# Attention then feed-forward on one core: weight loads spread behind normalizations, early v loads on another queue, and longer planned DMA times

## The chip, the cores and the metric

The kernel runs on one core of one Trainium2 chip. The metric is the device time of one execution in microseconds (us); the smaller the better. The engines are named as in the profile: PE is TensorE's matrix unit (PEld its weight loads), DVE is VectorE, ACT is ScalarE, POOL is GpSimd, SP is SyncE, which here only issues DMAs. ACTq, POOLq and SPq are their instruction queues. PSUM is the memory that matmuls write.

## What is computed

Attention with normalized q and k over 8 batches, 12 heads, 448 rows and 64 columns per head, and then a feed-forward layer with a gate over the 8 x 448 = 3584 rows of 768.

```
q, k, v: (8, 12, 448, 64)   w_in: (768, 2048)   w_out: (2048, 768)
q_n = q / sqrt(mean(q*q) + 1e-6) * g_q ;  k_n likewise with g_k
attn = softmax(q_n @ k_n.T / 8) @ v          # per batch and head
x = attn, heads side by side                 # (3584, 768)
h = x @ w_in
out = (h * clip(h + 3, 0, 6) / 6) @ w_out    # (3584, 768)
```

## The kernel before

**Tiling.** Two heads make a pair (index p, 48 in all; six pairs, HP, make one batch of x). Two pairs make a group (GP = 2), which is the unit of loading: `load_k` (L287), `load_q` (L278) and `load_v` (L294) bring one group's k, q or v, each as one large and one or two small DMAs, into one of NS staging buffers `kq_in` and `v_st`. The pairs of group 0 have k and q loaded one by one. The 448 rows of a head lie as three full tiles of 128 rows and a rest of 64; the rests of both heads share a tile.

**One pair's way.** `square` (L329) and `stats_sum` (L336) give the sums of squares, `stats_rstd` (L343) the factors, and `normalize` (L352) writes the scaled q and k as bf16 into `qk` (three tiles, NQ). Then q and k are transposed: for pairs below TD = 14 by PE into the PSUM tile `t_ps` (`transposes`, L364; k in its first half, q in the second), from which `put_k` and `put_q` (L381 to L388) copy them into `kq`; for later pairs by a transposing DMA on SP (`transposes_dma`, L376), after which ACT scales q (`scale_q`, L372). `burst` and `rests` (L390 to L405) make the scores, `expo2` (L407) their exponentials on ACT, `weigh` (L420) multiplies with v (cast to bf16 by `cast_v`, L359), and `divide` (L441) ends the softmax. The result is transposed into `xT`: below XD = 12 by PE (`x_out`, L462, into the PSUM tile `m` for the first batch) and `put_x` (L473), later by a transposing DMA (`x_out_dma`, L466).

**Feed-forward.** When the six pairs of a batch are in `xT`, the items `h` (`h_mm`, L478; six matmuls each, then `relu` on ACT and `gate` on DVE) and `y` (`y_mm`, L495; 16 matmuls each, a copy and a store) of that batch can run. One part of the first h item (`h_early`, L588) is spread over the pairs of the first batch.

**What sets the order.** A planner (`Plan`, L64) writes the whole order at build time. Each operation has a key (lower first), one or more engines with a planned duration, and dependencies. `run` (L140) steps through planned time; whenever an engine is free it gives it the ready operation with the lowest key. PE's matmuls of the feed-forward fill in between by `share` and `credit`. The engines and queues then execute exactly this order; on the chip an instruction waits for what it needs, and all behind it on its engine waits too. Planned times of DMAs are made of ISSUE (0.6 us on SP and ACT, 0.9 on POOL, per DMA), the bytes at RATE in one common pipe, and LAND until the data can be used. A transposing DMA is planned with 1.27 us of issue and a fixed time behind it (L95).

```
    def dma_transpose(self, key, size, fn, deps):
        return self.add(key, [("SP", 1270, fn)], deps, 2100, 1.4 * size)
```

**Loads.** k, q and v go through SP's queue (group 0's q through ACT's) in the order of their keys. A group's k and q wait, in the plan and on the chip, until the group NS before has been normalized, and its v until that one's v has been cast. The weights are nine DMAs on POOL's queue with a cast on the way: `load_w_in` (L312) for five ranges of columns, `load_w_out` (L316) for four. W_IN and W_OUT (L644) give for each the group whose v load it is planned behind: w_in 2, 2, 2, 3, 3 and w_out 5, 5, 6, 7. POOL also makes most normalizations (for all pairs but the first), most squares from pair 4 on and most casts of v.

Of the kernel before, what the change touches and what calls it, by code (L numbers as in the profile page):

```python
# [63 lines left out]
class Plan:  # L64
# [6 lines left out]
    ISSUE, LAND, RATE = {"SP": 600, "ACT": 600, "POOL": 900}, 1700, 270.0  # L71

    STEADY, SLACK, EARLY = 110e3, 500, 3000

    def __init__(self, share):
        self.free = {e: 0.0 for e in ("PE", "ACT", "DVE", "POOL", "SP", "pipe")}
        self.known, self.todo = [], 0
        self.lanes, self.row, self.banks = {"h": [], "y": []}, [], []
        self.share, self.credit = share, 0.0
# [15 lines left out]
    def dma_transpose(self, key, size, fn, deps):  # L95
        return self.add(key, [("SP", 1270, fn)], deps, 2100, 1.4 * size)
# [43 lines left out]
    def run(self):  # L140
        now = 0.0
        while self.todo or self.row or any(self.lanes.values()):
            soon = [t for t in self.free.values() if t > now]
            best = {}
            for op in self.known:
                t = op.time
                if op.bank is not None:
                    free = After(op.bank).end
                    if free is None:
                        continue  # L150
                    t = max(t, free + self.HOP)
                if t > now:
                    soon.append(t)
                    continue
                engine, ns, fn = min(op.ways, key=lambda w: max(self.free[w[0]], now) + w[1] * (
                    self.PRICE.get(w[0], 1.0) if op.key[0] >= self.FAIR else 1.0))
                if self.free[engine] <= now and (engine not in best or op.key < best[engine][0].key):
                    best[engine] = (op, ns, fn)
            if self.free["PE"] <= now and ("PE" not in best or self.credit < 0):
                if not self.row:  # L160
                    pick = self.next_item(now, soon)
                    if pick:
                        it, bank = pick
                        for lane in self.lanes.values():
                            if lane and lane[0] is it:
                                lane.pop(0)
                        it.bank, bank[1] = bank, it.out
                        self.row = list(it.ops)
                if self.row:
                    best["PE"] = (self.row[0], *self.row[0].ways[0][1:])  # L170
            if not best:
                now = min(soon)
            for engine, (op, ns, fn) in best.items():
                if op.key is None:
                    self.row.pop(0)
                    share = next((self.share[i] for i in range(0, len(self.share) - 1, 2)
                                  if it.place < self.share[i + 1]), self.share[-1])
                    self.credit = min(self.credit + ns * share, 2000.0)
                else:
                    self.known.remove(op)  # L180
                    self.todo -= 1
                    if engine == "PE":
                        self.credit = max(self.credit - ns, -2000.0)
                self.begin(op, engine, ns, fn, now)
        return now
# [3 lines left out]
def kernel(  # L189
# [11 lines left out]
    nc = tc.nc  # L201
# [13 lines left out]
    NS = 3  # L215
# [3 lines left out]
    TD = 14  # L219
    XD = 12  # L220
# [131 lines left out]
    def normalize(eng, p):  # L352
        eng.tensor_tensor(  # L353
            out=qk_r[p % NQ][:].rearrange("p a t h d -> p h (a t) d"), in0=raw(p, 2),
            in1=rstd_r[(p // GP) % 2][:, p % GP].rearrange("p h a t -> p h (a t)")
            .unsqueeze(3).to_broadcast([P, 2, 8, D]), op=A_MULT,
        )
# [6 lines left out]
    def transposes(p):  # L364
        for a in range(2):
            for t in range(4):
                nc.tensor.transpose(
                    t_ps[:, a, t * P:(t + 1) * P],
                    qk_r[p % NQ][:, a, t].rearrange("p h d -> p (h d)"), identity[:],
                )  # L370
# [10 lines left out]
    def put_q(eng, p):  # L381
        if eng is nc.scalar:
            eng.activation(out=qT_r[p % NK], in_=t_ps[:, 1, 0:S], func=COPY, scale=gprime[:])
        else:
            eng.tensor_scalar_mul(qT_r[p % NK], t_ps[:, 1, 0:S], gprime[:])

    def put_k(eng, p):
        copy(eng, out=kT_r[p % NK], in_=t_ps[:, 0, :])  # L388
# [67 lines left out]

    x_own = m_r[1][:].bitcast(BF16)
# [89 lines left out]
    V, G, A_ = nc.vector, nc.gpsimd, nc.scalar  # L547
    SINGLE = 4
# [6 lines left out]
    t_bank = []  # L555
    sc_last, ex_of, d_ops = {}, {}, []

    def x_stage(p):
# [10 lines left out]
        if p >= HP:  # L569
            xo[p].bank, xo[p].readers = t_bank, [px[p]]  # L570
# [69 lines left out]
    QA, VL, WK = 1, 1.5, 0  # L640
# [3 lines left out]
    W_IN = ((2, 0, 256), (2, 256, 256), (2, 512, 512), (3, 1024, 512), (3, 1536, 512))  # L644
    W_OUT = ((5, 0, 0, 8), (5, 0, 8, 8), (6, 1, 0, 8), (7, 1, 8, 8))
    w_loads, w_in_ops, w_out_ops = [], [], ([], [])
    for i, (after, *cols) in enumerate(W_IN):
        op = plan.dma((GP * after - WK, 3 + i), 1, NKT * P * cols[1] * 4, lambda cols=cols: load_w_in(*cols),
# [3 lines left out]
    for i, (after, *rows) in enumerate(W_OUT):  # L652
        op = plan.dma((GP * after - WK, 8 + i), 1, rows[2] * P * YC * 4, lambda rows=rows: load_w_out(*rows),
# [22 lines left out]
    for p in range(NPAIR):  # L676
        g = p // GP
        if p % GP == 0:
# [15 lines left out]
            lv_g[p] = plan.dma((p if g else VL, 2), 3, GP * kb, lambda p=p: load_v(nc.sync, p, GP), oldv)  # L694
            for i in range(1, GP):
                lv_g[p + i] = lv_g[p]
            for after, op in w_loads:
                if after == g:
                    lv_g[p].next.append(op)
            for i in range(GP):  # L700
                j, p0 = min(i, len(todo) - 1), p + i
                parts = []
                for part in ((0, 1) if p0 == 0 else (2,)):
# [10 lines left out]
                if g < SINGLE:  # L714
                    rstd_op[p0] = add((p0 - 2, 0), [("ACT", 430, lambda p0=p0: stats_rstd(
                        p0, (slice(None), p0 % GP)))], parts)
                else:
                    sums += parts
            if g >= SINGLE:
                rs = add((p - 2, 0), [("ACT", 450, lambda p=p: stats_rstd(p, (slice(None),)))],  # L720
                         sums[-GP:] + (norm_g[g - 2] if g >= 2 else []))
                for i in range(GP):
                    rstd_op[p + i] = rs
        ways = [("POOL", 1910, lambda p=p: normalize(G, p))]
        if p < 1:
            ways = [("DVE", 1240, lambda p=p: normalize(V, p))]
        nrm.append(add((p - 2, 4), ways, [rstd_op[p], at(tr, p - NQ)]))
        norm_g.setdefault(g, []).append(nrm[p])
        lv = lv_g
# [10 lines left out]
        else:  # L740
            free = sc_last.get(p - NK, [])
            tr.append(add((p - 1, 3), [("PE", 440, lambda p=p: transposes(p))],
                          [nrm[p], *free], 165))
            pq.append(add((p - 1, 3 if p == 0 else 0), [("DVE", 450, lambda p=p: put_q(V, p)), ("ACT", 640, lambda p=p: put_q(A_, p))],
                          [tr[p], mg]))
            pk.append(add((p - 1, 1), [("DVE", 420, lambda p=p: put_k(V, p)), ("ACT", 600, lambda p=p: put_k(A_, p))],
                          [tr[p]]))
            tr[p].bank, tr[p].readers = t_bank, [pq[p], pk[p]]
# [89 lines left out]
```

## Time and profile before

| | us |
|---|---|
| runs | 438.52, 441.98, 443.76 (median 441.98) |
| profiled execution | 439.38 |
| its span, first to last instruction | 437.6 |
| PE busy | 409.8 |
| ACT busy | 254.3 |
| DVE busy | 234.7 |
| POOL busy | 195.2 |
| bytes moved by DMA | 64.55 MB |

Busy time is what an engine's own instructions took; issuing a DMA, waiting and branching are not counted on SP's and ACT's queues. In a line of the timeline, the brackets give the engine's idle time before the instruction and what ended it. In the view by stretch, each engine has its busy time and, in parentheses, its number of instructions; then come the TensorE clock that was granted (1.00 is full speed), the mean busy share of the 16 DMA engines (some overlap makes it exceed 1), and GB/s. In the view of waits: who waited, for whom, us in total, times, longest us.

### The profile page before, as it was taken

What the parts mean: (1) busy time and instruction counts of PE and PEld (TensorE: products, weight loads), DVE (VectorE), ACT (ScalarE), POOL (GpSimd) and SP (SyncE); (2) the same over time, 40 slices, a digit from 0 to 9 for tenths busy, and PEclk for the clock granted to TensorE, in tenths of its full rate; (3) what the DMA queues carried; (4) which work ended last, traced back from release to release, by engine and by line L of the source; (5) the groups of instructions that cost most, each with busy time, mean ns of one, the idle gap of its engine ahead of it and who ended that gap; (6) DMA issues with size and microseconds to landing.
All of it is one profiled execution on the core that took longest, in us unless ns stands there. A gap on an engine that the chain in (4) does not pass through costs nothing.

```text
span 437.6 us, 8944 instructions
## 1 busy us (share of the span) xinstructions
PE 409.8 (94%) x3520; PEld 236.5 (54%) x3520; DVE 234.7 (54%) x492; ACT 254.3 (58%) x414; POOL 195.2 (45%) x146
## 2 busy tenths in 40 slices
PE   0677899999999998999999999999999999999997
PEld 0355565555566554555555555555565555555565
DVE  6486777766455557556466366344444253343322
ACT  3886887734877885968778587666643032132100
POOL 3697785596377776859676556311000000000000
PEclk9998999999999999999999999999999999999999
DMA  6999999995978898999999994333211201100022
GB/s 170 267 228 216 221 222 239 250 190 131 237 161 190 204 217 189 201 219 194 227 212 167 191 213 121 73 88 91 61 24 49 72 1 51 59 36 37 25 85 73
DMA packets 126506, 64.55 MB, mean 148 GB/s; under 512 B 77824, under 2 KB 123008, under 8 KB 126464
## 3 DMA queue, kind: packets, MB, share of 16 engines
q1 hardware_dynamic: 117488, 57.24, 57.5%
q0 software_dynamic: 8144, 6.29, 9.2%
q8 instruction: 27, 0.44, 0.4%
q10 hardware_dynamic: 832, 0.46, 0.4%
q14 instruction: 15, 0.12, 0.1%
HBM read 45.61 MB, written 11.01 MB: 129 GB/s over the span
## 4 chain that ended last, share of the span: by engine, by line
PE 82%; DMA 7%; ACT 3%; DVE 3%; SPq 2%; POOL 2%; issue 1%; ACTq 0%; POOLq 0%
PE m L479 18%; PE m L498 17%; PE t_ps L498 9%; PE t_ps L479 8%; PE av L435 7%; PE sc L395 6%; PE sc L498 6%; PE sc L479 4%; DMA kq_in<-in_k_dram 3%; DMA kq<-qk 3%; PE av L429 2%; DMA kq_in<-in_q_dram 2%; PE sc L402 2%; ACT eT L408 2%; DVE ssq L337 1%
## 5 line engine op out<-in xcount | busy, mean ns | idle before, releaser
L408 ACT ACTIVATE eT<-sc 128x896 bf16<-128x896 f32 x168 | 147.2, 915 | 42.2 <-PE sc L395 38.5
L498 PEld LDWEIGHTS <-gT 128*128 128x128 bf16 x912 | 85.5, 98 | 61.7 <-issue 8.9
L479 PE MATMUL m<-xT,w_in_sb 128*128 128x448 bf16 x486 | 109.9, 353 | 1.7 <-DVE xT L475 0.6
L479 PEld LDWEIGHTS <-w_in_sb 128*128 128x128 bf16 x768 | 70.7, 98 | 68.8 <-issue 12.0
L353 POOL TENSOR_TENSOR qk<-kq_in,rstd 128x1024 bf16<-128x1024 f32 x47 | 89.0, 1903 | 41.6 <-DMA kq<-qk 20.8
L498 PE MATMUL m<-w_out_sb,gT 128*128 128x384 bf16 (+1 forms) x480 | 87.3, 324 | 0.0
L334 POOL TENSOR_TENSOR sq<-kq_in 128x1024 f32<-128x1024 f32 x41 | 77.2, 1894 | 13.0 <-DMA kq_in<-in_q_dram 3.6
L490 DVE SCALAR_TENSOR_TENSOR gT<-t_sb,m 128x448 bf16<-128x448 f32 x81 | 49.9, 618 | 41.8 <-ACT t_sb L485 41.4
L485 ACT ACTIVATE t_sb<-m 128x448 f32<-128x448 f32 x81 | 44.1, 546 | 47.9 <-PE m L479 47.2
L337 DVE TENSOR_REDUCE ssq<-sq 128x16 f32<-128x1024 f32 (+1 forms) x49 | 58.1, 1190 | 9.5 <-POOL sq L334 7.5
L435 PE MATMUL av<-vaug,eT 128*128 128x65 bf16 x1152 | 59.6, 196 | 0.0
L435 PEld LDWEIGHTS <-eT 128*128 128x128 bf16 x1152 | 52.8, 100 | 7.2 <-issue 1.6
L498 PE MATMUL t_ps<-w_out_sb,gT 128*128 128x384 bf16 x256 | 46.9, 326 | 0.0
L395 PE MATMUL sc<-kq 64*128 64x448 bf16 x288 | 41.6, 363 | 4.0 <-ACT eT L408 2.5
L429 PE MATMUL av<-vaug,eT 128*128 128x130 bf16 x192 | 43.0, 224 | 2.4 <-ACT eT L408 1.2
L479 PE MATMUL t_ps<-xT,w_in_sb 128*128 128x448 bf16 x192 | 44.5, 352 | 0.7 <-DVE gT L490 0.7
L303 POOL CAST vaug<-v_st 128x512 bf16<-128x512 f32 x33 | 20.3, 620 | 55.0 <-PE av L435 46.6
L445 DVE RECIPROCAL rden<-av 128x4 f32<-128x4 f32 x96 | 17.3, 180 | 48.8 <-PE av L435 47.1
L446 DVE TENSOR_TENSOR xn<-av,rden 128x256 bf16<-128x256 f32 x96 | 40.7, 424 | 3.3
L374 ACT ACTIVATE kq<-kq,gprime 128x448 bf16<-128x448 bf16 x34 | 22.8, 670 | 14.2 <-DMA kq<-qk 14.2
L498 PE MATMUL sc<-w_out_sb,gT 128*128 128x384 bf16 (+1 forms) x176 | 29.1, 319 | 0.0
L485 ACT ACTIVATE t_sb<-t_ps 128x448 f32<-128x448 f32 x32 | 17.5, 547 | 19.7 <-PE t_ps L479 18.5
(50 smaller groups left out, 225.0 us busy)
## 6 DMA issues: line engine op xcount, KB each, us to landing
v_st<-in_v_dram SPq DMA_DIRECT2D x24, 384.0 KB, 4.7
kq_in<-in_k_dram SPq DMA_DIRECT2D x23, 384.0 KB, 4.5
kq_in<-in_q_dram SPq DMA_DIRECT2D x23, 384.0 KB, 4.8
out_dram<-y_sb SPq DMA_DIRECT2D x23, 384.0 KB, 2.6
w_out_sb<-in_moe_w_out_dram POOLq DMA_DIRECT2D x4, 768.0 KB, 19.1
w_in_sb<-in_moe_w_in_dram POOLq DMA_DIRECT2D x3, 768.0 KB, 16.2
out_dram<-y_sb SPq DMA_DIRECT2D x9, 192.0 KB, 2.7
v_st<-in_v_dram SPq DMA_DIRECT2D x48, 32.0 KB, 4.3
```

Source lines behind the costliest of these rows:

```text
L334: eng.tensor_tensor(out=sq, in0=x, in1=x, op=A_MULT)
L337: nc.vector.tensor_reduce(out=ssq_r[(p // GP) % 2][:, p % GP, :, which(part)].rearrange("p h a t -> p h (a t)"), in_=sq_r[m][:, :, which(p ...
L353: eng.tensor_tensor(out=qk_r[p % NQ][:].rearrange("p a t h d -> p h (a t) d"), in0=raw(p, 2), in1=rstd_r[(p // GP) % 2][:, p % GP].rearran ...
L395: nc.tensor.matmul(out=sc[:, h, 0:S], lhsT=kT_r[p % NK][rows, t * P:(t + 1) * P], rhs=qT_r[p % NK][rows], start=True, stop=True,)
L408: nc.scalar.activation(out=e2_r[d % NE][:, :, 0:S], in_=sc_r[i][:, :, 0:S], func=EXP, bias=0.0, scale=1.0,)
L429: nc.tensor.matmul(out=av, lhsT=rest[:, cols], rhs=va[:, 3].rearrange("p h d -> p (h d)"), start=True, stop=False, skip_group_check=True,)
L435: nc.tensor.matmul(out=av[:, h * W:(h + 1) * W], lhsT=e[t][h][:, cols], rhs=va[:, t, h], start=False, stop=(t == NT - 1 and h == 1), skip_ ...
L446: nc.vector.tensor_tensor(out=xn_r[p % NQ][:, t].rearrange("p n (h d) -> p n h d", h=2), in0=av4[:, :, :, 0:D], in1=rden.unsqueeze(3).to_b ...
L479: nc.tensor.matmul(out=m[:, 0:S], lhsT=w_in_sb[:, kt, f * P:(f + 1) * P], rhs=xT[:, kt, b % NX, x_slot(b)], start=(kt == 0), stop=(kt == N ...
L485: nc.scalar.activation(out=t[:], in_=m[:, 0:S], func=RELU, bias=0.5, scale=1.0 / 6.0,)
L490: nc.vector.scalar_tensor_tensor(out=gT[:, f, (b % 2) * S:(b % 2 + 1) * S], in0=t[:], scalar=1.0, in1=m[:, 0:S], op0=A_MIN, op1=A_MULT,)
L498: nc.tensor.matmul(out=m[:, 0:n], lhsT=gT[:, f, c0:c0 + P], rhs=w_out_sb[:, f, c:c + n], start=(f == 0), stop=(f == NFT - 1),)
```

## The change

- Each of the nine weight loads is planned and issued behind one pair's normalization: w_in behind pairs 3, 4, 5, 6 and 7, w_out behind pairs 7, 8, 9 and 10.
- v of groups 0 and 1 is issued by POOL rather than SP.
- Pair 0's normalization and factors are made for k and for q apart (SPLIT). For pairs 0 and 1 the transposes are two operations, and those of q go to the PSUM tile `m` that also takes the first batch's `x_out` (QB). Pair 0's k is copied by ACT and its q by DVE.
- There are four staging buffers rather than three.
- Planned times: a transposing DMA takes 3.5 us behind its issue rather than 2.1, a load lands 2.6 us behind the pipe rather than 1.7, the pipe has 300 bytes per ns rather than 270, and all engines start at 0.7 us.
- A new rule in `run`: an engine other than PE and SP is left idle when an operation whose key is lower by one or more becomes ready within half of the duration of the one that it would start. The choice between engines now also looks at when the operation becomes ready.

```diff
-    ISSUE, LAND, RATE = {"SP": 600, "ACT": 600, "POOL": 900}, 1700, 270.0
+    ISSUE, LAND, RATE = {"SP": 600, "ACT": 600, "POOL": 900}, 2600, 300.0
+    TURN = 3500
...
+    AHEAD, LOOK = 1, 0.5
...
-        self.free = {e: 0.0 for e in ("PE", "ACT", "DVE", "POOL", "SP", "pipe")}
+        self.free = {e: 700.0 for e in ("PE", "ACT", "DVE", "POOL", "SP", "pipe")}
...
-        return self.add(key, [("SP", 1270, fn)], deps, 2100, 1.4 * size)
+        return self.add(key, [("SP", 1270, fn)], deps, self.TURN, 1.4 * size)
...
+                engine, ns, fn = min(op.ways, key=lambda w: max(self.free[w[0]], now, t) + w[1] * (
+                    self.PRICE.get(w[0], 1.0) if op.key[0] >= self.FAIR else 1.0))
                 if t > now:
                     soon.append(t)
+                    ahead.append((engine, t, op.key))
                     continue
...
+            for engine, t, key in ahead:
+                if engine in best and engine != "PE" and engine != "SP":
+                    op, ns, _ = best[engine]
+                    if key[0] + self.AHEAD <= op.key[0] and t - now < self.LOOK * ns:
+                        del best[engine]
...
-    NS = 3
+    NS = 4
...
+    x_own = m_r[1][:].bitcast(BF16)
+    def t_place(p, a):
+        return x_own[:, 0:W4] if a and p < QB else t_ps[:, a, :]
...
-    W_IN = ((2, 0, 256), (2, 256, 256), (2, 512, 512), (3, 1024, 512), (3, 1536, 512))
-    W_OUT = ((5, 0, 0, 8), (5, 0, 8, 8), (6, 1, 0, 8), (7, 1, 8, 8))
+    W_IN = ((3, 0, 256), (4, 256, 256), (5, 512, 512), (6, 1024, 512), (7, 1536, 512))
+    W_OUT = ((7, 0, 0, 8), (8, 0, 8, 8), (9, 1, 0, 8), (10, 1, 8, 8))
...
-            lv_g[p] = plan.dma((p if g else VL, 2), 3, GP * kb, lambda p=p: load_v(nc.sync, p, GP), oldv)
+            veng, queue = (nc.gpsimd, "POOL") if g < VP else (nc.sync, "SP")
+            lv_g[p] = plan.dma((VK[g] if g < VP else p, 2), 3, GP * kb, lambda p=p, veng=veng: load_v(veng, p, GP), oldv,
+                               queue=queue)
...
-            for after, op in w_loads:
-                if after == g:
-                    lv_g[p].next.append(op)
...
-        nrm.append(add((p - 2, 4), ways, [rstd_op[p], at(tr, p - NQ)]))
+        ns = [normal(p, part, x) for part, x in zip((0, 1) if p < SPLIT else (2,), rstd_op[p])]
+        nrm.append(ns[-1])
         norm_g.setdefault(g, []).append(nrm[p])
+        for after, op in w_loads:
+            if after == p:
+                nrm[p].next.append(op)
+                op.deps[id(nrm[p])] = nrm[p]
...
+            ts = [add((p - 1, 3), [("PE", 440 if part == 2 else 220, lambda p=p, part=part: transposes(p, part))],
+                      [n, *free], 165) for part, n in ((0, ns[0]), (1, ns[-1]))[:2 if p < QB else 0] or ((2, nrm[p]),)]
+            tr.append(ts[-1])
...
+            ts[0].bank, ts[0].readers = t_bank, [pk[p]] + [pq[p]] * (p >= QB)
+            if p < QB:
+                ts[1].bank, ts[1].readers = x_own_bank, [pq[p]]
```

## Prediction

> **What bounds the kernel now.** The first view is the page: TensorE (PE) is busy for 409.8 of 437.6 us and the chain that ended last is 82% PE. No other engine passes 58%. PE's work does not change in this edit, so the time can only move by PE's idle time, 27.8 us, and the question is where that lies.
>
> ```profile
> span 437.6 us, 8944 instructions
> ...
> PE 409.8 (94%) x3520; PEld 236.5 (54%) x3520; DVE 234.7 (54%) x492; ACT 254.3 (58%) x414; POOL 195.2 (45%) x146
> ...
> PE   0677899999999998999999999999999999999997
> ...
> PE 82%; DMA 7%; ACT 3%; DVE 3%; SPq 2%; POOL 2%; issue 1%; ACTq 0%; POOLq 0%
> ```
>
> The second view, busy time by stretch, answers it. First column: length; second: PE busy; the last two: DMA share and GB/s.
>
> ```profile
> 0.00:9.38 9.38, 0.00 (x0) 0.00 (x1) 6.13 (x33) 3.87 (x6) 3.14 (x16) 1.00 0.59 161
> 9.38:52.41 43.03, 31.95 (x354) 20.20 (x355) 28.64 (x62) 33.20 (x54) 35.62 (x27) 0.96 1.08 233
> 52.41:150.00 97.59, 97.53 (x903) 56.62 (x903) 62.66 (x128) 67.47 (x111) 66.42 (x45) 1.00 0.97 203
> 150.00:232.00 82.00, 77.91 (x726) 43.90 (x724) 51.55 (x101) 62.33 (x105) 59.46 (x38) 1.00 0.99 210
> 232.00:435.00 203.00, 202.46 (x1541) 115.84 (x1538) 85.74 (x172) 87.42 (x140) 30.58 (x23) 1.00 0.33 79
> 435.00:437.60 2.60, 0.00 (x0) 0.00 (x0) 0.00 (x0) 0.00 (x0) 0.00 (x0) 1.00 0.13 41
> ```
>
> PE's idle time is 9.38 + 11.08 + 0.06 + 4.09 + 0.54 + 2.60 us. So there are two places where this edit can gain: the head, until the first batch's x is whole and feed-forward matmuls fill every gap (20.5 us), and the stretch 150 to 232 us (4.1 us). The rest is the last store.
>
> The third view is the chain of waits in order of time, for the head (start, length, what).
>
> ```profile
> 1.27 3.69 DMA kq_in<-in_q_dram
> 4.96 0.02 issue
> 4.98 0.59 SPq L298
> ...
> 9.52 4.37 DMA kq_in<-in_q_dram
> 13.89 0.33 issue
> 14.22 2.00 ACT sq L332 x2
> ```
>
> SP issues the first v loads (L298, L300) from 4.98 to 6.95, and only then k and q of the second group, whose squares start as q lands at 13.9. The timeline shows pair 0's two evacuations in turn, and the weights' loads in a row on POOL with what they do to SP's queue:
>
> ```profile
> 10.45 0.59 ACT L303 COPY kq<-t_ps 128x512 bf16<-128x512 bf16 x1 [1.38 <-PE t_ps L367]
> ...
> 11.07 0.45 DVE L385 TENSOR_SCALAR kq<-t_ps,gprime 128x448 bf16<-128x448 bf16 x1 [0.62 <-ACT kq L303]
> ...
> 28.72 2.54 POOL L313 DMA_DIRECT2D w_in_sb<-in_moe_w_in_dram  x3
> ...
> 36.97 4.77 SPq L292 DMA_DIRECT2D kq_in<-in_k_dram  x2
> ```
>
> For 150 to 232 us, the view of waits and that of the transposing DMA's line:
>
> ```profile
> ACT kq L374 <- DMA kq<-qk: 10.9, 8, 2.8
> ...
> POOL qk L353 <- DMA kq<-qk: 4.9, 4, 2.2
> ...
> DMA to landing us min/median/max: 3.1/3.6/6.0
> ```
>
> ACT and POOL work in a fixed order, and both stand for this DMA; behind ACT's 2.8 us (before 170.2) come the exponentials for which PE then waits.
>
> **The change, part by part.**
>
> *Pair 0 in two halves.* Today: sums 6.29 to 7.57 (two of 0.64), rstd to 8.06, one normalization of 1.23 to 9.33, eight transposes 9.38 to 10.41, k's copy (0.59), then q's (0.45), scores at 11.57. After: k's sum ends at 6.93 and its rstd (0.45) at 7.4; q's sum holds DVE until 7.57; half normalizations (0.62 each) end at 8.2 and 8.85; four transposes of k end at 8.75 and of q at 9.4; k's copy is hidden behind q's, which now lies in another PSUM bank, and q's ends at 9.9. Scores at 9.95: 1.6 us earlier. Added: two ACT instructions of 0.21, inside ACT's idle time.
>
> *v of groups 0 and 1 by POOL.* Six issues leave SP: 1.97 us (4.98 to 6.95) ahead of group 1's k and q, and 1.94 (10.17 to 12.11) ahead of group 2's. On POOL I price them by its nearest rows, 0.55 (gk_t) to 0.93 (w_out_sb): 3.3 to 5.6 us, hidden in the 8.4 us that POOL waited for v before its casts at 9.92 and 16.02; without that cover it would be late for pair 1's normalization by what exceeds it. But the bytes share the DMA engines. Between 0 and 5 us the share is 0.47 at 125 GB/s, between 5 and 10 0.76 at 217, afterwards 0.94 and up, to 267 GB/s. So 0.96 MB of room lies before 10 us, 3.6 us at that best rate, and v of one group is 0.46 MB (1.8 us). Group 1 gains 2.0 if v fits in that room and 0.2 if v of group 1 goes ahead of it entirely. Pair 0's 1.6 counts only as far as pairs 2 to 5 follow, so these two parts are one term, between 0 and -2.0. I take -1.5.
>
> *Each weight load behind one normalization.* Nine loads of 0.83 to 0.93 us stay nine on POOL; only their place moves. The first stands at 28.72 today; behind pair 3's normalization (the two at 21.17 end at 24.9) it comes 4 to 6 us earlier. POOL is full there (19.88 busy of 20 to 40 us), so every load delays the normalizations behind it by 0.85, pair 5's by at most 1.7; pair 4's ended at 28.8 and its first scores came at 34.0, which covers it. Gains: the first feed-forward matmul's wait for its columns (0.5), and part of the lower granted clock between 35 and 40 us (0.66 over 4.5 busy us costs 1.5), which follows the thin stretch before it (3.3 busy of 5); I count 0.7. The cost is traffic: k's small loads took 3.9 us to land before the weights and 12.8 beside them. Bounds -2.0 and +2.9 (weights at half rate for 5.7 us more); I take -1.2.
>
> *Four staging buffers.* SP's waits for a normalization ahead of k loads total 2.3 us over the whole run, none on the chain: 0. One more buffer's memsets (0.95 us by today's rows) lie in DVE's idle time before 6.29; without it the first sum starts up to 0.95 later.
>
> *Transposing DMAs planned longer.* The planner counts 1.27 of issue plus TURN: 3.37 us before, 4.77 after. Measured for kq: median 3.6, longest 6.0; for xT: median 3.0, longest 4.7. Today more than half of the kq DMAs land later than the fixed order expects, and each late one stops ACT or POOL with everything queued behind (exponentials; squares, then DVE's sums and the gates behind them, hence a PSUM bank freed late). After, all of xT and most of kq fit. Bounds: 0 and -4.1. I take three quarters, -3.1, because landings of 5 to 6 us still exceed it. Planning 1.4 us more per pair costs nothing while three qk tiles cover it (a pair takes 437.6 / 48 = 9.1 us).
>
> *Landing 2.6 for 1.7 us, rate 300 for 270, all engines starting at 0.7, and the holding rule.* The rule idles an engine for up to half an operation (0.46 us before an exponential) when a more urgent one is near. ACT has 19.7 idle us between 150 and 232, so 0. The times move places in the order, weighed in the third rival.
>
> **Sum.** 437.6 - 1.5 - 1.2 - 3.1 = 431.8 us span; around the span lie 439.38 - 437.6 = 1.8, so 433.6 against the profiled 439.38. That execution is 2.6 below the median 441.98; I add half of it: **435.0**. Its own range: 429 to 439.
>
> **Rivals.**
>
> *The transfers are the limit, and the head gains nothing.* From 10 us on the DMA share is 0.94 to 1.28, and the squares of groups 1, 2 and 3 start as q lands. Then only -3.1 is left: 437.6 - 3.1 + 1.8 + 1.3 = 437.6. Against it: the room before 10 us. The Trainium skill (DMA: Bandwidth & Descriptors, "Issuing engines are not separate DMA queues") says that starting DMAs from several engines saves only issue time, since all share the same 16 engines; by that rule the v term would be nothing wherever the queue is full, and the trace agrees with a full queue from 10 us on but not before.
>
> *Head only.* Late landings at 4.77 still stop ACT in the middle, or a stall that goes there leaves the next one: 437.6 - 2.7 + 1.8 + 1.3 = 438.0. For it: one late landing cascades (POOL at 158.7, DVE, PE at 164.2, SP, ACT at 170.2). Against it: only the longest landings exceed 4.77.
>
> *Slower: loads planned too early.* At 300 GB/s the planner expects 9 MB 3.3 us sooner than at 270 (30.0 against 33.3), only 0.9 of it given back by the later landing: 2.4 us too early against an order that already met 227 GB/s between 20 and 40. Weights starting 5.7 us earlier take half the rate, which puts k and q 2.9 us later. Together 5.3 us, in which ACT and POOL stand at squares of groups 3 to 5 ahead of the exponentials of pairs 2 to 5, with no feed-forward work yet. ACT's wait today is 1.5 (longest 0.8). The same rate shortens planned transposes when the queue is long, so the middle gains nothing: 441.98 + 5.3 = 447.3. It decides if q of group 4 lands over 3 us later than today's 31.7. Against it: four buffers and an SP freed of v put those loads about 4 us ahead.
>
> *It does not do what it says.* The reordered head trades one wait for another of its size: about 441.
>
> **How the numbers follow.** Forecast 0.52, transfers the limit 0.16, head only 0.11, slower 0.14, no effect 0.07. A measurement of this kernel tells about 1% from no change (the three runs span 1.2%). Below 437.6: nearly all of the forecast, half of the first rival and a little of the second, 0.60. Above 446.4: most of the slower case, 0.12. Between: 0.28. The range 427.5 to 443 takes in the first, second and fourth rivals and leaves out the slower one and an unlikely full gain.
>
> **What would show it.** Right: first scores near 10 us; group 1's q landed near 12.5; all weights' first columns before 37; the last xT copy of batch 0 (48.9 today) near 46; PE idle of 150 to 232 under 1.5 us and ACT's wait for kq under 4. Wrong: ACT or POOL waiting for kq_in by 2 us or more in the head, PE idle between 9 and 52 above 11, or new PE gaps after 90 us before a scaled q.

## The result, and the profile after

The changed kernel is slower: median 443.33 us (439.14 to 448.08, 20 runs) against 440.05 (437.43 to 444.09, 20 runs), ratio 1.0065, 95% interval 1.0044 to 1.0086. (The ratio leaves out disturbed executions, so it is not the quotient of the two medians.) The profiled execution has a span of 440.0 us against 437.6.

The page of the kernel after, its totals, PE's row of tenths and the engines' shares of the last chain:

```profile
span 440.0 us, 8938 instructions
...
PE 409.2 (93%) x3520; PEld 236.2 (54%) x3520; DVE 243.1 (55%) x512; ACT 250.6 (57%) x406; POOL 202.9 (46%) x148
...
PE   1477998799999999999999999999999999999997
...
PE 80%; DMA 10%; DVE 3%; POOL 2%; ACT 2%; issue 1%; SPq 0%; ACTq 0%; DVEq 0%
```

Behind the head, PE's row has one new dip, the 8 and the 7 in the seventh and eighth slices (66 to 88 us). The view by stretch of the kernel after, cut where it was cut for the kernel before, puts a number on it:

```profile
0.00:9.38 9.38, 0.00 (x0) 0.00 (x0) 7.05 (x43) 3.27 (x7) 5.86 (x14) 1.00 0.75 196
9.38:52.41 43.03, 31.38 (x371) 19.60 (x372) 34.40 (x72) 33.61 (x56) 35.90 (x25) 1.00 1.18 243
52.41:150.00 97.59, 92.51 (x853) 53.48 (x851) 64.26 (x128) 64.33 (x106) 71.35 (x46) 0.97 1.02 209
150.00:232.00 82.00, 80.27 (x755) 45.80 (x755) 50.09 (x97) 62.61 (x103) 58.10 (x40) 1.00 0.97 204
232.00:435.00 203.00, 203.00 (x1524) 115.54 (x1521) 86.61 (x172) 86.78 (x137) 31.71 (x25) 1.00 0.29 72
435.00:440.00 5.00, 1.99 (x25) 1.76 (x22) 0.71 (x2) 0.00 (x0) 0.00 (x0) 0.98 0.23 79
```

Length less PE's busy time gives PE's idle time:

| stretch, us | before | after | difference |
|---|---|---|---|
| 0 to 52.41 | 20.46 | 21.03 | +0.57 |
| 52.41 to 150 | 0.06 | 5.08 | +5.02 |
| 150 to 232 | 4.09 | 1.73 | -2.36 |
| 232 to the end | 3.14 | 3.01 | -0.13 |
| sum | 27.75 | 30.85 | +3.10 |

PE's busy time fell by 0.6 to 0.7, which leaves the 2.4 us of the span. So the middle gained what was hoped for, the head gained nothing, and a stretch that had had no gap at all now holds 5 us.

**The new gap** is at 76 us: 3.89 of the 5.08 us lie there, and one more of 1.0 ends the stretch. POOL's timeline around it, kernel after (in brackets the idle time before, and what the page takes for its end):

```profile
64.52 0.62 POOL L313 CAST vaug<-v_st 128x512 bf16<-128x512 f32 x1 [0.84 <-PE av L452]
73.23 1.89 POOL L344 TENSOR_TENSOR sq<-kq_in 128x1024 f32<-128x1024 f32 x1 [8.10 <-DVE gT L505]
75.07 0.62 POOL L313 CAST vaug<-v_st 128x512 bf16<-128x512 f32 x1
75.64 1.89 POOL L344 TENSOR_TENSOR sq<-kq_in 128x1024 f32<-128x1024 f32 x1
77.49 3.76 POOL L364 TENSOR_TENSOR qk<-kq_in,rstd 128x1024 bf16<-128x1024 f32 x2
```

and PE's, with PE and its clock in the stretches beside it:

```profile
79.45 1.04 PE L384 MATMUL t_ps<-identity,qk 128*128 128x128 bf16 x8 [3.89 <-POOL qk L364]
```

```profile
75.00:80.00 5.00, 1.11 (x9) 0.65 (x8) 2.26 (x4) 0.90 (x2) 5.00 (x5) 0.80 1.21 251
80.00:85.00 5.00, 5.00 (x46) 3.18 (x45) 2.38 (x6) 1.73 (x3) 1.25 (x1) 0.52 0.91 231
```

POOL stands idle for 8.1 us before a square of pair 14. The page names a gate of DVE that happened to end then; what the square had waited for is q of group 7, which landed at 73.1. The plan has that load land at 67.4 and the square start at 68.5, and so it put the square ahead of the normalizations of pairs 12 and 13. Not all of the 8.1 us is the load's: pair 12's sum, which frees the square's buffer, ended at 68.85 on DVE, so some 4.4 us are. Both squares of the group (1.89 us each) are made from 73.2 to 77.5, with a cast of v between them, and the normalizations stand behind them although their own factors were ready at 73.0. PE has nothing to do until the first of them ends. It waits 3.89 us, and the next 5 us run at a granted clock of 0.52, which by that number costs up to 5.00 x 0.48 = 2.4 us more.

A late load alone is not what makes a gap. In the same plan q of group 6 was to land at 47.1, and it landed at 58.5, 11.4 us later, without any new gap: its squares stand in the plan at 59.6, and they began at 59.93. Group 7's load missed by 5.7 us, and its square stands 1.1 us behind the planned landing.

The head and the middle, in the lines that answer to those shown of before. PE and DVE, kernel after:

```profile
9.54 0.61 PE L384 MATMUL t_ps<-identity,qk 128*128 128x128 bf16 x4 [9.54 <-DVE qk L364]
11.74 0.93 PE L412 MATMUL sc<-kq 64*128 64x448 bf16 x4 [0.99 <-ACT sq L342]
15.64 0.61 PE L384 MATMUL t_ps<-identity,qk 128*128 128x128 bf16 x4 [2.97 <-POOL qk L364]
```

```profile
5.12 1.15 DVE L548 MEMSET eT<- 128x128 bf16 x8
7.65 1.21 DVE L347 TENSOR_REDUCE ssq<-sq 128x8 f32<-128x512 f32 x2
10.00 1.12 DVE L556 SCALAR_TENSOR_TENSOR gprime<-gq_t,gk_t 64x1 f32<-64x1 f32 x2
```

The first sum comes at 7.65, not 6.29; the first scores at 11.74, not 11.57; pair 1's transposes at 15.64, not 13.44. The waits between 150 and 232 us, kernel after:

```profile
POOL qk L364 <- DMA kq<-qk: 18.8, 10, 3.4
...
ACT kq L391 <- DMA kq<-qk: 5.1, 3, 3.6
```

ACT's wait for the transposing DMA, which had held up the exponentials, fell from 10.9 to 5.1 us. POOL's rose from 4.9 to 18.8, and that cost PE little.

### The profile page after: what moved, and what is told of

The parts are those of the page before. It is cut to its first block, busy times and chain, and to the rows that moved or that the text cites. A ratio compares the mean times of both kernels' runs of the same rounds, so it can differ in the third digit from the quotient of the medians.

```text
span 440.0 us, 8938 instructions
## 1 busy us (share of the span) xinstructions
PE 409.2 (93%) x3520; PEld 236.2 (54%) x3520; DVE 243.1 (55%) x512; ACT 250.6 (57%) x406; POOL 202.9 (46%) x148
## 4 chain that ended last, share of the span: by engine, by line
PE 80%; DMA 10%; DVE 3%; POOL 2%; ACT 2%; issue 1%; SPq 0%; ACTq 0%; DVEq 0%
PE m L513 19%; PE m L494 16%; PE t_ps L494 8%; PE t_ps L513 8%; DMA v_st<-in_v_dram 8%; PE av L452 7%; PE sc L513 7%; PE sc L412 6%; PE sc L494 4%; DMA kq<-qk 3%; PE av L446 2%; PE sc L419 2%; ACT eT L425 1%; POOL qk L364 1%; POOL sq L344 1%
## 5 line engine op out<-in xcount | busy, mean ns | idle before, releaser
L494 PE MATMUL m<-xT,w_in_sb 128*128 128x448 bf16 x474 | 106.1, 354 | 1.1 <-DMA w_in_sb<-in_moe_w_in_dram 0.5
L513 PE MATMUL m<-w_out_sb,gT 128*128 128x384 bf16 (+1 forms) x528 | 94.1, 321 | 0.0
L344 POOL TENSOR_TENSOR sq<-kq_in 128x1024 f32<-128x1024 f32 x43 | 80.9, 1894 | 15.4 <-DVE gT L505 9.1
L500 ACT ACTIVATE t_sb<-m 128x448 f32<-128x448 f32 x79 | 42.9, 545 | 48.7 <-PE m L494 47.5
L313 POOL CAST vaug<-v_st 128x512 bf16<-128x512 f32 x35 | 21.7, 622 | 57.5 <-PE av L452 54.5
L494 PE MATMUL t_ps<-xT,w_in_sb 128*128 128x448 bf16 x204 | 47.3, 353 | 0.0
L513 PE MATMUL t_ps<-w_out_sb,gT 128*128 128x384 bf16 x208 | 38.6, 326 | 0.0
L505 DVE SCALAR_TENSOR_TENSOR gT<-t_sb,t_ps 128x448 bf16<-128x448 f32 x34 | 21.1, 620 | 30.7 <-ACT t_sb L500 30.6
L462 DVE RECIPROCAL rden<-av 128x4 f32<-128x4 f32 x96 | 17.2, 179 | 36.2 <-PE av L452 35.2
L513 PE MATMUL sc<-w_out_sb,gT 128*128 128x384 bf16 x176 | 30.1, 326 | 0.0
```

The source lines that it names most:

```text
L344: eng.tensor_tensor(out=sq, in0=x, in1=x, op=A_MULT)
L494: nc.tensor.matmul(out=m[:, 0:S], lhsT=w_in_sb[:, kt, f * P:(f + 1) * P], rhs=xT[:, kt, b % NX, x_slot(b)], start=(kt == 0), stop=(kt == N ...
L500: nc.scalar.activation(out=t[:], in_=m[:, 0:S], func=RELU, bias=0.5, scale=1.0 / 6.0,)
L505: nc.vector.scalar_tensor_tensor(out=gT[:, f, (b % 2) * S:(b % 2 + 1) * S], in0=t[:], scalar=1.0, in1=m[:, 0:S], op0=A_MIN, op1=A_MULT,)
L513: nc.tensor.matmul(out=m[:, 0:n], lhsT=gT[:, f, c0:c0 + P], rhs=w_out_sb[:, f, c:c + n], start=(f == 0), stop=(f == NFT - 1),)
```

## The experiments

Two explanations stood against each other: that the planned times of loads (2600 and 300) make the plan promise data too early, and that the cause lies elsewhere, in the order itself, the holding rule, v on POOL, the four buffers or the weights. All ratios are to the kernel before on the same chip.

| run | us | ratio (95%) | PE idle, 52 to 150 | 150 to 232 |
|---|---|---|---|---|
| after | 443.33 | 1.0065 (1.0044 to 1.0086) | 5.08 | 1.73 |
| less w_out traffic | 435.45 | 0.9925 (0.9894 to 0.9957) | 0.21 | 0.80 |
| square behind normalizations | 437.87 | 0.9974 (0.9948 to 1.0) | 1.37 | 0.82 |
| v by SP | 441.2 | 1.0055 (1.0025 to 1.0085) | 0.58 | 4.35 |
| before + 3500 | 435.76 | 0.9946 (0.992 to 0.9971) | 0.22 | 1.58 |
| no holding rule | 450.09 | 1.0273 (1.0247 to 1.0298) | 1.59 | 3.88 |
| old load times | 434.83 | 0.9929 (0.9906 to 0.9952) | 1.13 | 0.53 |
| before + split + 3500 | 437.33 | 0.9963 (0.9938 to 0.9988) | 0.54 | 0.65 |
| the same, four buffers | 442.91 | 1.0115 (1.0084 to 1.0147) | 2.36 | 2.56 |
| rate 270 alone | 441.39 | 1.0001 (0.9967 to 1.0036) | 4.71 | 0.57 |
| before + load times | 447.32 | 1.0156 (1.0117 to 1.0196) | 3.06 | 6.22 |
| old load times, v by SP | 435.06 | 0.9883 (0.9853 to 0.9913) | 1.16 | 0.10 |
| old load times, old weights | 437.33 | 0.9942 (0.9917 to 0.9966) | 0.86 | 0.00 |

**The same order, less traffic.** Each w_out load brings only two of its eight rows of tiles.

```
 def load_w_out(...):
+    n = 2
 y_mm:  rhs=w_out_sb[:, f // 8 * 8 + f % 2, c:c + n]
```

> The changed kernel in its own order and plan, but each of the four w_out loads brings 2 of its 8 row tiles (the y matmuls use those two over and over), so some 4.7 MB less of weights move between 43 and 81 us; the output is therefore not the reference's. Theory A (POOL stands at the square of pair 14 because q of group 7 lands at 73.1, later than the order expects, and pair 12's normalization is queued behind it): q of group 7 lands before 68, POOL's 8.1 us of waiting falls under 3, PE's 3.9 us before 79.4 and the low clock behind it go, time 4 to 5 us below the changed kernel, so 0.993 to 0.997 of the kernel before. Rival B (the 3.9 us come from the order alone, DVE's sums held back for gates, whatever the loads do): PE still waits 3 us or more there, time as the changed kernel, 1.005 or more.

The stretch from 52 to 150 us of this kernel, and POOL's longest wait between 30 and 100 us that the page puts down to a load:

```profile
52.41:150.00 97.59, 97.38 (x921) 56.39 (x918) 70.29 (x140) 70.97 (x118) 75.45 (x49) 1.00 0.86 199
```

```profile
POOL sq L345 <- DMA kq_in<-in_q_dram: 3.8, 1, 3.8
```

q of group 7 lands at 65.1 rather than 73.1, ahead of its planned 67.4, and the gap is gone with every instruction in the order that was slow. The 3.8 us are in front of the same square of pair 14, but they are not a wait for its q, which had landed: the square began at 69.24, when DVE had finished pair 12's sum.

```profile
67.95 1.21 DVE L348 TENSOR_REDUCE ssq<-sq 128x16 f32<-128x1024 f32 x1
```

So the order as such is not the fault; that the load comes later than the order assumes is.

**The square behind the normalizations.** The waiting square is put behind the normalizations that it held up.

```
-    src + ([squares[m - 2]] if m >= 2 else []) + nrm[:1]
+    src + ([squares[m - 2]] if m >= 2 else []) + nrm[:1] + (norm_g[6] if g == 7 else [])
```

> The changed kernel with one more planned dependency: the squares of pairs 14 and 15 come behind the normalizations of pairs 12 and 13. The loads stay as they are. Theory A: POOL's wait for q of group 7 now lies behind the two normalizations, PE does not wait for pair 12's transposes by more than 1 us, time 3 to 5 us below the changed kernel (0.995 to 1.000 of the kernel before). Rival B, or a stall that goes on to the next user: PE's idle time between 52 and 150 us stays above 3 us and the time at 1.005 or more.

q of group 7 lands no sooner (75.5), but POOL no longer stands for it: it normalizes meanwhile, and the squares follow without a wait. POOL's timeline:

```profile
75.09 3.76 POOL L364 TENSOR_TENSOR qk<-kq_in,rstd 128x1024 bf16<-128x1024 f32 x2 [3.28 <-ACT rstd L358]
78.81 3.75 POOL L344 TENSOR_TENSOR sq<-kq_in 128x1024 f32<-128x1024 f32 x2
```

PE's longest wait in the stretch is 0.87. The late load costs nothing by itself; the work queued behind it did.

**v of groups 0 and 1 back on SP.**

```
-    QA, VP, VK = 1, 2, (-1, 1)
+    QA, VP, VK = 1, 0, (1.5, 1)
...
-    lv_g[p] = plan.dma((VK[g] if g < VP else p, 2), 3, GP * kb, ...
+    lv_g[p] = plan.dma((p if g else 1.5, 2), 3, GP * kb, ...
```

> The changed kernel with the v loads of groups 0 and 1 on SP again (keys as in the kernel before); with that the planner puts the fill of eT back on POOL. Theory A (the head's gain was lost because v on POOL took DMA time from pair 1's k and q and pushed the 1.2 us fill onto DVE ahead of pair 0's sums): pair 0's first sum starts near 6.4 rather than 7.65, first scores near 10.3 rather than 11.7, pair 1's k and q land near 7.9 rather than 9.9, PE's idle time up to 52 us falls by 2 or more. Rival C (the head is set by the loads of groups 1 and 2 whatever the queue): first scores earlier, but idle time up to 52 us within 1 us of the changed kernel's 21.0. The time depends also on whether the stall near 76 us stays, which this kernel does not address.

The first sum comes at 6.54 and pair 1's k and q land at 7.9 rather than 9.9: with v on POOL it was v's bytes that came first. PE's idle time up to 52.41 falls from 21.03 to 18.63, as Theory A asked, but the clock granted between 9.38 and 52.41 was 0.88, and the total is within the interval of the kernel after. This order has no stall at 76; it has another, on PE:

```profile
169.54 0.37 PE L412 MATMUL sc<-kq 64*128 64x448 bf16 x2 [2.66 <-ACT eT L425]
```

Just before it ACT had stood 4.62 us for a transposing DMA, with the exponentials behind.

Every edit of a plan moves all that follows, so total times of two orders say little about the edit unless the stalls are read too.

**The transposing DMA's time alone**, in the kernel before.

```
-    return self.add(key, [("SP", 1270, fn)], deps, 2100, 1.4 * size)
+    return self.add(key, [("SP", 1270, fn)], deps, 3500, 1.4 * size)
```

> The kernel before with the planned time behind a transposing DMA at 3.5 instead of 2.1 us, nothing else. Theory A (this part alone works as predicted): PE's idle time between 150 and 232 us falls from 4.1 to under 2, no new one, time 0.992 to 0.996 of the kernel before. Rival D (the gain of the middle in the changed kernel is luck of another order): idle time there 3 to 5 us, or as much elsewhere, time 0.998 to 1.005.

```profile
150.00:232.00 82.00, 80.42 (x767) 45.31 (x766) 51.83 (x104) 64.74 (x107) 58.25 (x39) 1.00 1.00 207
```

PE's idle time there (above) falls from 4.09 to 1.58, ACT's wait for kq from 10.9 to 3.0, and nothing new opens before 150: 2.9 us off the median of 438.67 beside it, 2.4 by the ratio.

**No holding rule**, in the kernel after.

```
-    AHEAD, LOOK = 1, 0.5
+    AHEAD, LOOK = 1, 0.0
```

> The changed kernel without the rule that leaves an engine idle (LOOK 0); the planned times of loads stay. The order is another one: DVE takes the sums of pairs 12 and 13 early and POOL normalizes both pairs ahead of any square of pair 14 or 15. Theory A, in its refined form (the stall near 76 us needs two parts: the rule that holds DVE's sums back until pair 12's normalization stands behind pair 14's square, and the load of group 7 planned 5 to 6 us early): PE's wait for pair 12's transposes is gone (under 0.5 us). ACT now squares pair 14, and as its load is still planned too early (57 us), ACT stands there for it, so a new stall of PE of 3 us or more near 58 to 75 is likely: time 1.000 to 1.010. Rival E (the rule is harmless, the planned load times alone make the stall): PE still waits 3 us or more for pair 12's transposes.

The wait at 76 goes, but the kernel becomes slower still, and by more than expected. PE's line and POOL's wait, 30 to 100 us:

```profile
51.78 0.27 PE L446 MATMUL av<-vaug,eT 128*128 128x130 bf16 x1 [9.49 <-DVE xn L463]
```

```profile
POOL sq L344 <- DMA kq_in<-in_q_dram: 9.8, 1, 9.8
```

It is the same thing elsewhere: q of group 5 was planned for 34.6 and landed at 46.0, and the square that waited for it held up POOL, then DVE (a sum), then PE. The rule is not the cause; it only decided where the early promise bites.

**The load times put back**, all else as after.

```
-    ISSUE, LAND, RATE = {"SP": 600, "ACT": 600, "POOL": 900}, 2600, 300.0
+    ISSUE, LAND, RATE = {"SP": 600, "ACT": 600, "POOL": 900}, 1700, 270.0
```

> The changed kernel with LAND 1700 and RATE 270 as before; the holding rule and all else stay. q of group 7 is then planned for 71.6 rather than 67.4, close to the 73.1 measured, but pair 12's normalization still stands behind pair 14's square. Theory A: POOL's wait for it shrinks from 8.1 to under 4 us and PE's stall near 76 from 3.9 to under 2; the head is as in the changed kernel; time 0.999 to 1.004. Rival E' (the load times do not matter, only the place in the order): PE's stall stays 3 us or more, time 1.005 or more.

```profile
52.41:150.00 97.59, 96.46 (x908) 56.58 (x904) 63.94 (x128) 65.21 (x108) 68.05 (x46) 1.00 0.99 202
150.00:232.00 82.00, 81.47 (x737) 45.28 (x737) 52.15 (x101) 64.73 (x105) 59.28 (x41) 1.00 0.96 202
```

Neither POOL nor ACT waits for a load between 40 and 100 us any more. From 1.0065 to 0.9929 is 1.36% of 440, some 6 us, for two numbers in the planner; 0.999 at best had been expected. Its plan has q of group 7 land at 71.6, and it landed at 67.3.

**The load times alone**, put into the kernel before (2600 and 300, nothing else).

> The kernel before with the planned load times of the change alone (LAND 2600, RATE 300). Theory A (planning loads too early harms any order): a wait for kq_in of 2 us or more on ACT or POOL between 20 and 100 us that the kernel before does not have, time 1.004 to 1.015. Rival F (it harms only an order that also has four buffers, weights spread and holding): no such wait, time within 0.3% of the kernel before.

It loses 1.56%, 6.9 us. The middle of this kernel:

```profile
150.00:232.00 82.00, 75.78 (x706) 42.30 (x703) 45.60 (x90) 58.58 (x94) 58.84 (x40) 0.96 0.95 205
```

Idle time rises by 3.00 between 52 and 150 us and by 2.13 between 150 and 232. Before 100 there are new waits for loads: POOL's square of group 7 waits 3.2 us and that of group 8 4.8 us (the page names a v load there, but a square reads k and q; q of group 8 was planned for 77.8 and landed at 84.9), and ACT waits 2.3 us for q. The largest single gap of PE is another:

```profile
168.67 0.91 PE L402 MATMUL sc<-kq 128*128 128x448 bf16 x2 [4.48 <-ACT eT L408]
```

It stands behind ACT's waits of 3.52 and 2.30 us for transposing DMAs; POOL had waited 1.24 us for q ahead of a normalization there, and how much of this gap is the loads' stays open. Taking the two numbers away from the new kernel and giving them to the old one agree in sign and in size, the size in part by luck.

**One of the two numbers**: the rate back at 270, landing left at 2.6.

> The changed kernel with RATE 270 and LAND still 2600: the planned landings are those of the kernel before plus 0.9 us. It tells which of the two numbers does the harm. If it is the rate (q of group 7 is planned for 74.2 at this rate, later than the 73.1 measured in the changed kernel): no wait of POOL or ACT for kq_in above 3 us between 40 and 100 us, PE's idle time between 52 and 150 us under 2, time 0.990 to 0.997 of the kernel before. If it is the longer landing: time 1.003 or more.

That the rate alone was to blame did not come true: the ratio is 1.0001, between the two, with a stall of another group. ACT and PE:

```profile
56.67 1.06 ACT L342 ACTIVATE sq<-kq_in 128x1024 f32<-128x1024 f32 x1 [5.02 <-DMA kq_in<-in_q_dram]
```

```profile
59.68 0.35 PE L494 MATMUL m<-xT,w_in_sb 128*128 128x448 bf16 x1 [4.22 <-DVE gT L505]
```

q of group 6 was planned for 49.9 and landed at 56.5. How much is due to either number stays open; a longer landing time shifts the order too, so one number can't be read off alone.

**The head's pieces.** The kernel before with the split of pair 0 and 3500 (old load times, no holding rule, three buffers, v by SP, weights behind pairs 5, 5, 5, 7, 7 and 7, 7, 11, 13, as near the old places as pairs allow), and then the same with four buffers:

```
-    NS = 3
+    NS = 4
```

> The kernel before with three parts of the change: the planned time behind a transposing DMA (3.5 us), pair 0 in two halves with q in its own PSUM tile, and planned start at 0.7 us. Loads of v by SP, weights behind the v loads of groups 2, 3, 5, 6 and 7 as far as their keys allow, three buffers, old load times, no holding. Theory A: the middle gains as in the run with the longer planned time alone (ratio 0.995), and the head gains what the split is worth when nothing is put on DVE ahead of it: first scores near 10.2 rather than 11.6, PE's idle time up to 52 us 19 or less; time 0.989 to 0.995. Rival C (the head is paced by the loads of groups 1 and 2): idle time up to 52 us within 0.7 of the 20.5 before, time 0.994 to 0.998.

> The same kernel with four staging buffers instead of three. If the fourth buffer is worth nothing by itself (as I costed it), the time is within 0.3% of that run and its extra memsets show as up to 0.95 us on DVE before the first sum. If it lets loads crowd the weights or be planned ahead of what the queue can do, a wait for kq_in of 2 us or more appears on ACT or POOL between 40 and 80 us and the time is 0.5% or more above it.

With the split, the first transposes and scores come at 8.26 and 10.98, 1.1 and 0.6 us earlier than before, and PE's idle time up to 52.41 is 20.65 against 20.46. The ratio, 0.9963, is no better than that of 3500 alone. Four buffers then cost 1.5%. PE's and ACT's lines, and POOL's wait:

```profile
45.09 0.49 PE L412 MATMUL sc<-kq 64*128 64x448 bf16 x2 [2.80 <-ACT eT L425]
```

```profile
43.17 1.06 ACT L342 ACTIVATE sq<-kq_in 128x1024 f32<-128x1024 f32 x1 [3.01 <-issue]
```

```profile
POOL sq L344 <- DMA kq_in<-in_q_dram: 5.0, 2, 3.1
```

The page gives no cause for ACT's 3.01 us, but q of group 5 landed at 43.0, where the plan had 35.2, and PE's 2.80 us follow from it. POOL's 3.1 us are for q of group 6 (planned 49.0, landed 59.6); DVE's sum and a gate stand behind, and PE's gap of 2.15 us at 64. So the plan starts squares of loads too early here even with the old load times. The kernel called old load times has four buffers too and no such wait. It differs by the holding rule, the spread weights and v on POOL. The two kernels below show no such stall either; one has v on SP as here and the other has the weights as here. Of the three differences only the holding rule is common to all that are free of it, so the rule is the likely remedy; it wasn't tried alone.

**Old load times with v on SP**, and **old load times with the weights near their old places** (the two edits shown or named above, each on top of the old load times).

> The changed kernel with the old load times, and v of groups 0 and 1 on SP (the fill of eT then goes back to POOL). On a base without the stall this isolates that part. Theory A: PE starts 1.1 us or more earlier than 9.54, its wait for pair 1's transposes falls from 3.3 to 1.7, idle time up to 52 us falls from 21.5 to 19.5 or less, time 0.4% or more below the run with the old load times (under 0.989). Rival C: the head's idle time changes by under 1 us, time within 0.3% of that run (0.990 to 0.996).

> The changed kernel with the old load times, and the weights behind pairs 5, 5, 5, 7, 7 (w_in) and 7, 7, 11, 13 (w_out), close to where they stood before. If spreading them is worth what I took (1.2 us) or more, this run is 0.3% or more above the run with the old load times (0.996 or more), with PE waiting for w_in_sb. If it is worth nothing: 0.990 to 0.995.

The first has the lowest ratio here, 0.9883, ahead of both kernels; but its own median and span (435.06 and 433.2 us) are those of the old load times alone (434.83 and 433.1), the runs of the kernel before beside it were slower, and the intervals overlap. That it is the faster of the two is not shown. Its PE idle time up to 52.41 is 21.55, the other's 21.49: that v comes from SP moves pair 0's scores to 10.89 and leaves the head as long as it was. The second has PE waiting for weights:

```profile
41.75 1.30 PE L494 MATMUL m<-xT,w_in_sb 128*128 128x448 bf16 x3 [2.84 <-DMA w_in_sb<-in_moe_w_in_dram]
```

Its ratio, 0.9942, lies where the spread was expected to be worth nothing. Against the runs of the kernel before beside each, old load times save 3.7 us with the spread weights and 2.5 without: 1.2 us for the spread by medians, 0.6 by the ratios, with intervals that overlap. Nor are these quite the old places: the first weights are issued at 33.4, in the kernel before at 28.7, and PE waited 0.5 us for them there rather than 2.84. What the spread is worth is not shown.

## Why the prediction was wrong, and where it was right

**The step that failed** is the last part of the sum: "Landing 2.6 for 1.7 us, rate 300 for 270 [...] so 0". It measured 6 us (taken away from the kernel after) and 6.9 us (given to the kernel before, where part may be due to transposing DMAs). The reason given for 0 was ACT's idle time and the holding rule; but the cost of a planned time is not in the engine that waits, it is in what the fixed order has put behind it. In the kernel after that was two normalizations behind two squares: 3.89 us without work for PE, and up to 2.4 us of lower clock.

**The third rival had the mechanism and the wrong place.** It said that loads planned too early would make ACT and POOL stand at squares. It looked for that in the head, groups 3 to 5, with q of group 4 over 3 us later than 31.7. That load came at 28.5, earlier, by SP's freed time and the fourth buffer, as its "against" said. The stand came at group 7, where the plan was 5.7 us ahead of the chip (67.4 planned, 73.1 landed). Its price of 5.3 us was near the 6 measured, though made of other things. It also held that "the middle gains nothing", which was wrong: 4.09 fell to 1.73. It was given a chance of 0.14 because I compared the planned rate with what the head met; I should have followed planned against likely landing times load by load, group after group, and looked at what stood behind each square.

**The transposing DMAs** were right in kind and nearly in size: -3.1 forecast, -2.4 to -2.9 measured alone, -2.36 of PE's idle time in the kernel after. One reading behind it was wrong. "3.37 us before" left out that the planner also sends a transposing DMA's bytes through its pipe: 367 KB by its count at 270 bytes per ns, which makes 4.06 us the least for kq. So not more than half of the kq DMAs but 6 of 34 took longer from issue to landing than planned in the kernel before, and none with 3500 alone.

**Pair 0 and v** (-1.5 forecast, nothing measured). Scores were to come at 9.95 and came at 11.74. Three terms were missing. POOL issues v from 2.88 to 6.8 and no longer has time for the fill of eT, which the plan gave to DVE (1.15 us). The fourth buffer's memsets were laid in "DVE's idle time before 6.29", which the fill had taken; both together put the first sum 1.36 later. And the products for gprime, 0.31 for two in DVE's free time in the kernel before, took 1.12 and stood ahead of q's copy; why they were longer I can't say. As to v itself: pair 1's k and q landed 2 us later, since v shared the engines with them, and q of group 1 at 14.6 (14.15 before), though issued sooner.

**The first rival's claim about the head held**: whatever came earlier in pair 0, PE's idle time up to 52.41, with what a lower clock cost there (busy time times one less the clock), is 21.0 in the kernel after, 21.7 before, 22.6 with v on SP and 23.1 with the split alone: transposes that start 1.1 us sooner leave no trace in it. The Trainium skill (DMA: Bandwidth & Descriptors, "Issuing engines are not separate DMA queues") says that starting transfers from several engines saves issue time only, as all run on the same 16 engines. The trace agrees: two us of SP's issue time were saved, and group 1's q came 0.45 us later. I had weighed that rule only from 10 us on and trusted the room before; v's bytes took the room from pair 1's k and q. The rival's time, 437.6, did not come, for want of the load times.

**The weights** (-1.2 forecast) stay open: 0.6 to 1.2 us measured between the two kernels with old load times, within the noise. The first columns landed at 32.5 rather than 37.1, but PE's wait for them is 0.5 us in both kernels. The head's lower clock (0.96) went to 1.00, yet it did so too in the kernel before with 3500 alone, whose weights stand where they stood, and it stayed 0.96 with the square behind the normalizations, whose weights are spread; so the 0.7 us counted for it can't be put down to the weights. "Four staging buffers: 0" was too bold for a plan: up to 1.5% in one order, nothing seen in another.

Put together with sizes by the ratios, -2.4 (transposes), 0 (pair 0 and v) and +6.0 (load times) make +3.6 us. The ratio is 0.65% above 1, or 2.9 us; the 0.7 between is less than the width of the intervals, and all that is left for the weights. As orders differ among the kernels, that the sum closes so well is partly luck. The median of three runs was 1.9 us above that of twenty, so the step toward it (+1.3) was too much as well.

Of the signs named in advance, the first weights' landing (before 37, came at 32.5) and the last xT copy of the first batch (near 46, came at 46.2) spoke for the forecast; idle time of 1.73 us between 150 and 232 (under 1.5 was asked) and ACT's 5.1 us for kq (under 4) nearly so. First scores (near 10, came at 11.74) and group 1's q (near 12.5, came at 14.6) spoke against it, and so did "PE idle between 9 and 52 above 11", at 11.65, though the kernel before has 11.08 there already. The gap that decided came at 76 us, between the two places that were named to be watched, the head and what lies behind 90.

## What to carry to other kernels

In a schedule written out ahead for in-order engines, a load that is planned too early can cost everything queued behind its consumer: compare each load's planned landing with the measured one, and both with the place of the first instruction that needs it. Where that instruction stands well behind the landing, a miss of 11 us cost nothing; where it stands 1 us behind, one of 5.7 us left PE without work for 3.89 us. A load planned 4.3 us too late (q of group 7 with the old load times) made no gap. When an edit to a planner bundles several numbers, try them one by one, both added to the old kernel and removed from the new, and compare stalls and their places rather than totals, for each edit reshuffles the rest. Where the transfers set the pace, as in this head, work made earlier at the very start was not time gained.

## What the runs showed of the hardware that was not expected

The granted clock fell not only behind long stalls. After PE's 3.89 us without work it was 0.52 for 5 us, after 4.22 us in the kernel with rate 270 it was 0.66 for 5 us. The Trainium skill (TensorE: Matmul & The Clock Gate, "What's actually happening") has a clock of one half after an idle window of some 3.4 us, and these two stalls agree. But in the kernel before, 35 to 40 us at 0.66 followed a stretch with no gap above 0.5 us and 3.3 us busy of 5; with v on SP the clock was 0.50 at 30 to 35 us, behind gaps of 1.11 and 0.47 us. A thin stretch of short gaps can cost as much as a stall, and need not: in the kernel before with 3500 alone, PE is busy for 3.20 of the 5 us up to 35, and the next 5 us have a clock of 1.00.

When a load lands is far less certain than its size suggests. The v load issued at 61.98 in the kernel after landed 14.5 us later, where the median of its kind is 4.8. q of group 7 landed at 65.1, 67.3, 73.1 or 75.5 us in four kernels that differ in order or in the weights' traffic, a spread of 10 us, while the planner's two settings moved its planned landing by 4.2.
